# Layer 2 of one expert by seven block products in the first tile, with a new order of the first tile's steps

## The chip, the cores and the metric

The kernel runs on one core of a Trainium2 chip. A core has TensorE (PE, matmuls; its weight loads are listed as PEld), VectorE (DVE), ScalarE (ACT), GpSimd (POOL) and SyncE (SP, which here only starts DMA transfers). The engines run their own instruction streams in order and meet through semaphores; 16 DMA engines move data between HBM and the on-chip memory SBUF. PE writes its results to PSUM, in banks, from which DVE or ACT must take them ("evict") before the bank is used again.

The metric is the device time of one execution in microseconds (us). Before the change it is 486.61 us, the median of three runs (486.33 to 486.74).

## The reference

Linear attention is followed by a mixture of four expert networks, weighted by probabilities:

```python
def _attn_ref(q, k, v):                       # q, k, v: (8, 8, 576, 64)
    q_p, k_p = (phi(q), phi(k))               # phi(x) = elu(x) + 1
    kv = np.einsum('bhsd,bhse->bhde', k_p, v)
    z = np.sum(k_p, axis=2)
    num = np.einsum('bhsd,bhde->bhse', q_p, kv)
    den = np.einsum('bhsd,bhd->bhs', q_p, z)[..., None] + 1e-06
    return (num / den).astype(np.float32)
...
def _moe_ref(x, domain_probs, w1, w2):        # x: (4608, 512), w1: (4, 512, 1024), w2: (4, 1024, 512)
    p = domain_probs / (domain_probs.sum(-1, keepdims=True) + 1e-09)
    for e in range(E):
        h = np.maximum(x @ w1[e], 0.0)
        out += p[:, e:e + 1] * (h @ w2[e])
    return out.astype(np.float32)
```

The attention's output, with the heads side by side, is x: 8 batches of 576 tokens, 512 numbers each.

## The kernel before

**Tiles.** Of each batch 512 tokens form one tile; the 64 tokens left of each of the eight batches ("left") form a ninth. Tile 0 is batch 0. For each tile and each expert e, layer 1 (512 to 1024 numbers, then relu) and layer 2 (1024 to 512, scaled by the probability and summed over the experts in `acc`) are computed. While a tile is in the experts, the attention of the next batch is prepared.

**Block products.** From tile 1 on both layers are done by seven products of half-size blocks in place of the eight that a plain product of 2 by 2 blocks needs, at the price of sums of blocks. Layer 1: class `Block`, steps p1 to p7 with c22, for each half d of the hidden numbers; token sums `token_sum` (ts), weight sums `weight_sums` (s, on DVE). Layer 2: `layer2_product` (steps m, L786 on: seven products for each half of 256 tokens, 14 in all, four 128x256 matmuls each), with sums of the hidden numbers `hidden_sum` (hs, eight for a tile and expert, on POOL) and of the weights `weight_sums2` (t, four for an expert, on DVE). t.3 and s.3 change a block of the weights in place, and hs.2 a block of h.

**Tile 0** is different. Layer 1 of expert 0 is plain (`layer1_half`, steps L), layer 1 of experts 1 to 3 is by block products. Layer 2 is plain for all four experts: `layer2_part`, steps `y{e}.{ns}{part}`, four token groups ns of four parts each; a part is two matmuls of 128x512, and each group ends with one eviction into `acc`.

**Names of steps.** `p6.031` is step p6 of tile 0, expert 3, half 1; `y3.20` is expert 3, group 2, part 0; `m10.21` is tile 1, expert 0, product 2, token half 1; `hs10.03` is tile 1, expert 0, half 0, sum 3. `b1.` and `b2.` mark the attention of batches 1 and 2: k, q, v (ACT), km, qm (DVE), lk, lq, lv (the left rows), kv, qT, nd, xT, nl, xl (PE and an eviction).

**Loads.** q, k and v of batch 0 come by SP and ACT (lq0 to lq3, lk0 to lk3, lv0 to lv3), the probabilities by SP (lpr0 for tile 0, lpr for the rest; `emit_probs`, pr0 and pr1, norms them on DVE). POOL starts the transfers of the weights, which also cast them from fp32 to fp16: w1er is part r of w1 of expert e (four of 256 KB for expert 0, else two of 512 KB), w2er the same of w2; and those of batch 1 (k0 to k3, q0 to q3, v0 to v3, rk and rv for the left rows). Batch 2 comes by SP: `b1.load{i}` are its first six parts (load0 k0, load1 k1, load2 v0, load3 k2, load4 v1, load5 k3), `b2.load{i}` those after (load0 v2, load1 v3, load2 q0). `b1.loadlq` is the left q of batch 1, `b1.next` the left rows of batch 2. The raw parts share a pool of six buffers (`NRAW = 6`, tag "raw").

**The order** of all steps is written out by hand up to tile 1 in `CFG["EARLY"]`; after that steps go by a position (`put_at`). A step with several stages (a PE stage, then its eviction) stands in the list once for each: `advance` runs the step's generator on by one stage. The order of the list is the order in each engine's stream and in each engine's DMA queue.

Of the kernel before, what the change touches and what calls it, by code (L numbers as in the profile page):

```python
# [80 lines left out]
    "KC": ('AA', 'AV', 'VA', 'AA'),  # L81
    "XT": ('AA', 'AA', 'AV', 'AV'),
    "CUT": (((0, 2, 4),) * 4, ((0, 2, 4),) * 4),
    "MOVE": {"m83.10": 512.0, "m83.11": 512.0, "m83.20": 512.0, "m83.21": 512.0, "m82.41": 528.0},
    "WARM": (14, 3, 2, 1, 5),
    "BANK": {'qT0': 'py', 'qT1': 'b', 'nd00': 'py', 'nd00+': 'b', 'kv2': 'py', 'xT00': 'b', 'kv3': 'b', 'nd10+': 'b', 'L00': 'b', 'L10': 'py', 'nd01': 'b', 'xT01': 'py', 'nd11+': 'b', 'L20': 'e', 'L30': 'e', 'L01': 'e', 'L11': 'py', 'L21': 'py', 'L31': 'b', 'b1.qT3': 'py', 'b1.nd30': 'py', 'b1.nd21': 'b', 'b1.q1': 'b', 'b1.qT1': 'py', 'b1.nd01': 'py', 'b1.xT2': 'b', 'b1.nd11': 'py', 'b1.xT0': 'b'},
    "EARLY": (
        "lq2 lq3 lq0 lk0 qe0 ql0 ql3 qm0 kl0 lk1 lpr0 ke0 km0 qe2 ql2 qm2 lv0 ke1 kl1 km1 warm0 qT0 lv1 lk2 qe3 qm3 warm1 qT2 qT0 vc0 w100 warm2 kv0 vc1 qT2",
        "warm3 kv1 lk3 kv0 kv0 kl2 kv1 kl3 w102 kv1 nd01 lv3 nd01 warm4 xT11 xT01 ke2 km2 qT3 w103 vc3 lv2 ke3 vc2 nd00 w101 km3 xT01 w110 xT11 w111 kv3 k3 kv2",
        "qT3 lq1 nd00 qe1 xT00 w200 kv3 rk1 ql1 kv3 kv2 w201 qm1 L01 kv2 nd11 xT10 L31 qT1 v0 nd11 rv0 xT00 xT10 L10 xT21 rk0 xT21 v1 xT31 L11 qT1 xT31 nd10",  # L90
        "L01 L01 rv1 L31 w120 nd10 ts0.2 L00 ts0.0 xT30 ts0.1 xT20 L31 s0.0 L20 xT20 L30 xT30 L10 L10 L00 L00 L30 ts0.3 L30 p1.011 s1.0 p1.010 L11 L20 p1.010",
        "p2.010 s1.1 L20 w121 p2.010 p1.011 L21 L21 L21 s1.2 p6.010 p5.010 w210 L11 s1.3 p6.011 y0.30 p2.011 p6.010 p7.010 w211 p7.010 s0.1 p6.011 c22.010 v2",
        "y0.31 y0.00 p4.010 p2.011 y0.32 y0.33 p5.011 b1.k3 k0 pr0 y0.33 t0.0 t0.1 b1.km3 p7.011 p7.011 c22.011 y0.01 y0.02 y0.03 p4.010 b1.lk y0.20 y0.03 k2",
        "p4.011 s0.2 p3.010 p4.011 p3.011 y0.21 y0.10 y0.22 p3.010 y0.11 b1.v0 q1 k1 p1.021 y0.23 p1.021 p3.011 p1.020 s2.0 y0.12 v3 p2.021 b1.lv p1.020 t0.3",
        "s2.1 p2.020 s2.3 s2.2 y0.23 b1.v1 q0 t0.2 p6.020 p6.020 y0.13 p6.021 y0.13 y1.20 p7.020 y1.21 p2.020 p5.020 p7.020 w130 p2.021 y1.22 y1.23 t1.0 y1.10",
        "w131 p5.021 b1.v2 q3 b1.lkm y1.11 p6.021 b1.k0 b1.k2 b1.k1 w220 t1.1 t1.2 p7.021 y1.12 p7.021 c22.020 p3.020 y1.23 b1.v3 b1.km0 p4.020 p4.020 y1.00",
        "y1.01 q2 w221 y1.13 p4.021 b1.km2 b1.km1 b1.kv c22.021 p3.021 y1.02 y1.03 p1.030 p4.021 b1.q1 y1.30 y1.13 b1.load1 p1.031 b1.q0 p3.020 y1.31 p3.021",
        "p1.030 b1.qm1 b1.qT1 y1.32 y1.03 b1.qm0 s3.0 p1.031 w231 b1.qT0 s3.1 p2.030 y1.33 p6.030 b1.kv b1.qT0 p6.031 p2.031 b1.nd00 b1.nd01 b1.q3 p6.030 s3.3",
        "y1.33 p7.030 b1.loadlq p2.030 p5.030 b1.qm3 b1.qT3 p6.031 p7.030 w230 b1.qT1 b1.nd01 p7.031 p4.030 b1.qT3 s3.2 c22.030 b1.nd10 b1.nd11 b1.nd00 p2.031",
        "p3.030 b1.nd11 b1.nd10 p7.031 y2.00 y2.01 b1.nd30 p5.031 p4.031 p4.030 b1.next b1.nd31 b1.nd30 y2.20 b1.load0 b1.xT0 b1.lq b1.lqm b1.nd31 b1.q2 b1.qm2",  # L100
        "y2.21 b1.xT3 y2.02 c22.031 p4.031 b2.load2 y2.03 s0.3 b1.xT3 b1.qT2 y2.22 y2.23 b2.load1 b1.xT1 b1.load4 b1.load3 b1.load2 b1.qT2 b1.nd20 p3.031",
        "b1.xT1 p3.030 b1.nd21 y2.03 b1.xT0 b1.nd20 b1.nd21 y2.23 y2.10 y2.11 ts1.0 p1.101 p1.101 b1.load5 t1.3 b2.load0 t2.0 b1.xT2 y2.12 y2.13 b1.xT2 b2.k1",
        "ts1.1 lpr y2.30 y2.31 p1.100 p1.100 y2.32 y2.33 p3.031 p2.101 y3.20 y2.13 b2.km1 p6.100 b2.lk p2.100 t3.0 b2.load4 p2.101 p6.101 p6.100 p2.100 b2.lv",
        "ts1.2 p7.100 ts1.3 p7.100 b2.k0 y3.21 p5.100 y2.33 y3.22 t2.1 p4.100 y3.23 p6.101 p5.101 p4.100 p7.101 y3.30 c22.100 p3.100 b2.ones b1.qTl b2.v3 y3.00",
        "y3.01 p7.101 p4.101 b2.k2 b2.lkm y3.23 b2.km0 b2.load3 c22.101 b2.v1 y3.31 p3.100 t2.3 y3.32 p4.101 hs10.00 p3.101 b2.load5 y3.02 p1.110 b2.km2 y3.33",
        "p3.101 y3.03 b2.k3 b2.v0 b2.km3 b2.v2 b2.kv p1.110 y3.33 b2.load10 m10.21 b2.load7 p1.111 y3.03 y3.10 hs10.01 b1.qTl b2.q0 y3.11 p6.110 hs10.10",
        "hs10.02 y3.33 pr1 y3.12 y3.03 p1.111 m10.21 b2.q3 b2.load11 b2.qm0 y3.13 m10.51 hs10.11 p2.110 p6.111 p6.110 b2.q2 p2.111 m10.51 b2.qm3 y3.13 p2.110",
        "p6.111 t2.2 p7.110 m10.11 p5.110 m10.20 p7.110 b2.qm2 m10.11 b2.q1 c22.110 hs10.03 hs10.12 p7.111 m10.61 b2.qm1 t3.1 m10.20 p4.110 p4.110 p3.110",
        "p3.110 m10.50 p1.120 t3.2 b1.nl p2.111 p5.111 b3.load1 hs10.13 m10.61 m10.31 m10.31 m10.50 m10.10 p7.111 p4.111 b2.kv hs11.00 m10.10 m10.71 p1.120",
        "c22.111 t3.3 p6.120 m10.71 b2.lq b2.lqm p4.111 m10.60 b1.nl hs11.01 p3.111 p1.121 p6.120 y3.13 b2.load6 b2.qT m10.41 b2.qTl m10.60 m10.30 p2.120",  # L110
        "b2.nd1 p3.111 m10.41 m10.30 p7.120 b2.nd1 b2.nd0 hs11.10 y3.23 m10.70 m10.70 m11.21 hs11.11 p2.120 p5.120 m11.21 m10.40 p7.120 p4.120 hs11.03 p1.121",
        "p6.121 m11.20 m11.51 c22.120 p3.120 m10.40 b2.nd0 m11.20 p4.120 b3.k1 m11.50 m11.51 b3.km1 m11.11 p6.121 p2.121 m11.50 b2.nd1 b2.nd2 p3.120 p7.121",
        "m11.11 b2.nd3 b2.nd2 p1.130 hs11.02 p7.121 hs12.00 p2.121 b3.load0 b2.nd3 hs11.13 m11.10 m11.10 b2.next m11.61 m11.61 p5.121 p1.130 c22.121 p2.130",
        "m11.60 m11.31 p3.121 p6.130 m11.31 p4.121 b2.nd3 p6.130 hs11.12 m11.71 p4.121 p3.121 hs12.01 hs12.02 p2.130 m11.60 b2.nd4 hs12.10 p7.130 m11.71",
        "hs12.12 b2.nd5 p7.130 b2.nd2 b2.load8 m11.30 p5.130 p1.131 p1.131 m11.41 ts2.0 b2.nd4 b2.nd5 b2.nd5 m11.30 m11.41 m11.70 hs12.03 p6.131 p6.131 m12.20",
        "m11.70 m11.40 hs12.11 b3.ones c22.130 p4.130 p3.130 b1.xl p7.131 m12.21 p4.130 p7.131 m12.20 m11.40 b2.nl p2.131 b3.v0 p1.200 m12.21 b2.nl m12.50",
        "p2.131 m12.50 m12.51 p4.131 hs12.13 m12.51 ts2.1 p3.130 m12.10 m12.10 m12.11 m12.11 p5.131 p1.200 ts2.3 m12.60 m12.61 ts2.2 m12.60 b3.k0 m12.61",
        "c22.131 hs13.00 b2.load9 p4.131 p6.200",
    ),
}  # L120

# [2 lines left out]
def kernel(  # L124
# [642 lines left out]
        else:  # L767
            nc.vector.tensor_tensor(out=b12, in0=b22, in1=b12, op=AO.subtract)

    def hidden_sum(h, hs, i):  # L770

        a11, a21 = h[:, :, 0, 0:NH], h[:, :, 0, NH:NT]
        a12, a22 = h[:, :, 1, 0:NH], h[:, :, 1, NH:NT]
        if i != 2:
            hs[i] = pm.tile([P, 2, NH], FP16, tag=f"hs{i}", bufs=2, name=f"hs{i}")
        if i == 0:
            nc.gpsimd.tensor_tensor(out=hs[0], in0=a21, in1=a22, op=AO.add)  # L777
        elif i == 1:
            nc.gpsimd.tensor_tensor(out=hs[1], in0=hs[0], in1=a11, op=AO.subtract)  # L779
        elif i == 2:  # L780
            nc.gpsimd.tensor_tensor(out=a21, in0=a11, in1=a21, op=AO.subtract)  # L781
        else:
            nc.gpsimd.tensor_tensor(out=hs[3], in0=a12, in1=hs[1], op=AO.subtract)  # L783
# [220 lines left out]
    with tc.manual_schedule(  # L1004
# [46 lines left out]
        for e in range(E):  # L1051
            h0 = hT if e == 0 else [None, None]
            for d in range(2) if e else ():
                put_block(CFG["BLK"][2 * e - 2 + d], 0, e, d, h0)
            for i, pos in enumerate(CFG["L2P"][e]):
                put_at(pos, f"y{e}.{i // 4}{i % 4}", layer2_part, 0, e, i // 4, h0, i % 4, 4)
            for i in range(4):
                put_at(CFG["WS1"][e][i], f"s{e}.{i}", weight_sums, e, i)
                put_at(CFG["WS2"][e][i], f"t{e}.{i}", weight_sums2, e, i)
        base = CFG["BLK"][6]  # L1060
        units = [(j, e) for j in range(1, NTILES) for e in range(E)]
        for n, (j, e) in enumerate(units):
            h, hss = [None, None], [[None] * 4, [None] * 4]
            at = base + 2 * NSLOT * n
            for d in range(2):
                put_block(at + d * NSLOT, j, e, d, h)
            at += 2 * NSLOT + LAG

            def hsum(d, i, hT=h, hss=hss):
                hidden_sum(hT[d], hss[d], i)  # L1070

            for d in range(2):
                for i in range(4):
                    put_at(at + HSUM[d][i], f"hs{j}{e}.{d}{i}", hsum, d, i)
            order = L2ORD
            if n == len(units) - 1:
                order, at = (1, 2, 5, 6, 7, 3, 4), at + NSLOT
            for m in range(14):
                put_at(at + L2AT[m], f"m{j}{e}.{order[m // 2]}{m % 2}", layer2_product, j, e, h, hss, order[m // 2], m % 2)
# [71 lines left out]
```

## Time and profile before

| what | value |
|---|---|
| median of 3 runs | 486.61 us |
| span of the profiled execution, first to last instruction | 484.6 us |
| mean granted TensorE clock | 0.998 |
| PE, PEld busy | 474.4 us, 407.2 us |
| DVE, ACT, POOL busy | 377.3, 332.2, 358.3 us |
| bytes moved by DMA | 53.67 MB, of these 11.47 MB by POOL's queue (q0) |
| last landing of a weight part | 64.9 us |

The page gives the busy time of each engine, as a sum and in 40 slices, the DMA queues, the chain of work that ended last, and groups of instructions with their mean time and the idle time before them. The trace behind it can be asked for stages ("windows": busy time of each engine in a stretch), for the timeline of one engine (start, duration, engine, line, operation, out<-in; in brackets the idle time before and what ended it), and for waits. Line numbers are those of the kernel. A busy PE is not PE at its peak, as matmuls overlap; the distance from one start to the next is 0.109 us for a 128x256 matmul and 0.215 us for a 128x512 one.

### The profile page before, as it was taken

The page shows a single profiled execution, that of the slowest core. Times are in us where ns is not written, and L with a number is a line of the kernel's source. Part 1 is how long each engine was busy: PE and PEld are TensorE (multiplying, and loading weights), DVE is VectorE, ACT ScalarE, POOL GpSimd, SP SyncE. Part 2 cuts the span into 40 slices and gives each one's busy share as a digit, 9 for nine tenths or more (in the row PEclk, how much of TensorE's full clock was granted, in tenths as well). Part 3 has the DMA queues.
Part 4 walks back from the last instruction along what each step waited for, and adds up shares of the span by engine and source line. Part 5 has one row for each costly group of instructions (what it writes and reads, how often), then busy time and mean ns, then how long its engine had stood idle before and what let it go on. Part 6 is the DMA issues. An engine that isn't in the chain of part 4 may idle for free.

```text
span 484.6 us, 12013 instructions
## 1 busy us (share of the span) xinstructions
PE 474.4 (98%) x4565; PEld 407.2 (84%) x4565; DVE 377.3 (78%) x794; ACT 332.2 (69%) x662; POOL 358.3 (74%) x343
## 2 busy tenths in 40 slices
PE   6999999999999999999999999999999999999996
PEld 2766766898889888998889888988898888888885
DVE  5768987987868895888679886988687756775676
ACT  5689989956895599649884888478944565446530
POOL 5566044689966986789777977697769877987775
PEclk9999999999999999999999999999999999999999
DMA  8999987543445154523552446323221020002003
GB/s 293 216 217 254 233 204 201 134 109 88 123 144 111 42 156 150 120 53 115 172 135 56 114 133 157 77 77 106 69 59 28 7 93 2 1 0 89 2 1 87
DMA packets 79945, 53.67 MB, mean 111 GB/s; under 512 B 45152, under 2 KB 72608, under 8 KB 79888
## 3 DMA queue, kind: packets, MB, share of 16 engines
q1 hardware_dynamic: 69760, 40.43, 30.4%
q0 software_dynamic: 8896, 11.47, 12.3%
q10 hardware_dynamic: 1232, 1.02, 0.6%
q8 instruction: 35, 0.57, 0.5%
q14 instruction: 22, 0.18, 0.1%
HBM read 45.16 MB, written 9.44 MB: 113 GB/s over the span
## 4 chain that ended last, share of the span: by engine, by line
PE 90%; DMA 5%; DVE 2%; ACT 2%; issue 0%; POOL 0%; SPq 0%; ACTq 0%; DVEq 0%
PE py L810 38%; PE pb L868 24%; PE pe L868 18%; PE py L715 4%; DMA w<-in_moe_w_dram 2%; PE ph L655 1%; PE psum_nd L472 1%; DMA rawq<-in_q_dram 1%; DMA rawb<-in_q_dram 1%; DMA out_dram<-acc 1%; PE psum_kv L444 1%; PE pb L810 1%; PE pe L810 1%; DVE acc L706 0%; PE psum_nl L490 0%
## 5 line engine op out<-in xcount | busy, mean ns | idle before, releaser
L706 DVE SCALAR_TENSOR_TENSOR acc<-py,p_sb,acc 128x256 f32<-128x256 f32 (+1 forms) x382 | 182.2, 488 | 42.7 <-PE py L810 39.1
L852 DVE CUSTOM_DVE_ANT_0 h<-pe,u 128x512 f16<-128x512 f32 x140 | 96.1, 688 | 45.3 <-PE pe L868 28.0
L868 PEld LDWEIGHTS <-w 128*128 128x128 f16 x1120 | 108.9, 98 | 16.2
L777 POOL TENSOR_TENSOR hs<-h 128x512 f16<-128x512 f16 x64 | 74.7, 1167 | 56.9 <-DVE h L852 51.0
L810 PEld LDWEIGHTS <-h 128*128 128x128 f16 x1024 | 99.6, 98 | 12.2 <-issue 0.9
L810 PE MATMUL py<-w,h 128*128 128x256 f16 x744 | 106.4, 273 | 0.5 <-ACT acc L704 0.5
L879 ACT COPY u<-pb 128x512 f32<-128x512 f32 x140 | 82.4, 591 | 29.7 <-PE pb L868 27.8
L779 POOL TENSOR_TENSOR hs<-hs,h 128x512 f16<-128x512 f16 x64 | 74.1, 1157 | 26.8 <-PE py L810 24.3
L868 PEld LDWEIGHTS <-s 128*128 128x128 f16 x840 | 81.2, 98 | 12.6 <-DVE s L747 0.7
L868 PE MATMUL pb<-tt,w 128*128 128x256 f16 x560 | 83.8, 273 | 0.0
L810 PEld LDWEIGHTS <-hs 128*128 128x128 f16 x768 | 74.4, 98 | 8.8 <-issue 0.2
L783 POOL TENSOR_TENSOR hs<-h,hs 128x512 f16<-128x512 f16 x64 | 74.2, 1159 | 0.8 <-POOL h L781 0.5
L781 POOL TENSOR_TENSOR h<-h 128x512 f16<-128x512 f16 x64 | 74.6, 1165 | 0.1
L810 PE MATMUL py<-t,hs 128*128 128x256 f16 x496 | 74.1, 273 | 0.0
L901 ACT ACTIVATE h<-pe 128x512 f16<-128x512 f32 x70 | 41.9, 599 | 41.1 <-PE pe L868 40.5
L894 ACT COPY pe<-pb 128x512 f32<-128x512 f32 x70 | 40.0, 571 | 41.3 <-PE pb L868 15.8
L922 ACT ACTIVATE h<-pb 128x512 f16<-128x512 f32 x70 | 41.8, 599 | 6.3 <-PE pb L868 6.2
L868 PE MATMUL pb<-tt,s 128*128 128x256 f16 x280 | 41.9, 273 | 0.2 <-DVE s L747 0.2
L868 PE MATMUL pe<-tt,s 128*128 128x256 f16 x280 | 42.0, 273 | 0.0
L868 PE MATMUL pe<-xT,s 128*128 128x256 f16 x248 | 37.1, 273 | 0.0
L868 PE MATMUL pb<-xT,w 128*128 128x256 f16 x248 | 37.1, 273 | 0.0
L868 PE MATMUL pe<-xT,w 128*128 128x256 f16 x248 | 37.0, 273 | 0.0
(133 smaller groups left out, 594.6 us busy)
## 6 DMA issues: line engine op xcount, KB each, us to landing
out_dram<-acc SPq DMA_DIRECT2D x32, 256.0 KB, 2.5
w<-in_moe_w_dram POOLq DMA_DIRECT2D x14, 512.0 KB, 10.6
rawb<-in_k_dram SPq DMA_DIRECT2D x24, 256.0 KB, 3.1
rawb<-in_q_dram SPq DMA_DIRECT2D x24, 256.0 KB, 2.7
rawb<-in_v_dram SPq DMA_DIRECT2D x24, 256.0 KB, 2.8
w<-in_moe_w_dram POOLq DMA_DIRECT2D x4, 256.0 KB, 5.8
rawb<-in_k_dram POOLq DMA_DIRECT2D x4, 256.0 KB, 10.5
rl<-in_q_dram SPq DMA_DIRECT2D x16, 64.0 KB, 3.1
```

The source lines that it names most:

```text
L706: nc.vector.scalar_tensor_tensor(out=acc, in0=ps, scalar=pscal, in1=acc, op0=AO.mult, op1=AO.add)
L777: nc.gpsimd.tensor_tensor(out=hs[0], in0=a21, in1=a22, op=AO.add)
L779: nc.gpsimd.tensor_tensor(out=hs[1], in0=hs[0], in1=a11, op=AO.subtract)
L781: nc.gpsimd.tensor_tensor(out=a21, in0=a11, in1=a21, op=AO.subtract)
L783: nc.gpsimd.tensor_tensor(out=hs[3], in0=a12, in1=hs[1], op=AO.subtract)
L810: nc.tensor.matmul(out=ps, lhsT=lhsT(k), rhs=rhs[:, k], start=first and k == 0, stop=k == FH - 1, skip_group_check=True,)
L852: nc.vector._custom_dve(TENSOR_ADD_SAT, out=out, in0=ps, in1=u, s0=BIG, s1=0.0)
L868: nc.tensor.matmul(out=ps[:, kk], lhsT=lk(kc), rhs=rhs[:, kc], start=first and kk == 0 and kc == 0, stop=kc == 1, skip_group_check=True,)
L879: nc.scalar.copy(u, self.b)
L894: nc.scalar.copy(self.e5, self.b)
L901: nc.scalar.activation(self.h[:, :, 0, 0:NH], self.e5, AF.Relu)
L922: nc.scalar.activation(self.h[:, :, 1, 0:NH], self.b, AF.Relu)
```

## The change

Layer 2 of expert 3 in tile 0 is done by the 14 block products m03.* with eight sums hs03.* on POOL in place of the sixteen plain steps y3.*. `hidden_sum` takes the pair of halves and d, so that it can be called for both. `EARLY` is replaced as a whole, and reaches some 50 entries further; in it the loads have another order, and `lpr` and `pr1` stand early in tile 0.

```diff
+    "SEVEN": (3,),
...
     "EARLY": (
-        "lq2 lq3 lq0 lk0 qe0 ql0 ql3 qm0 kl0 lk1 lpr0 ke0 km0 qe2 ql2 qm2 lv0 ke1 kl1 km1 warm0 qT0 lv1 lk2 qe3 qm3 warm1 qT2 qT0 vc0 w100 warm2 kv0 vc1 qT2",
-        "warm3 kv1 lk3 kv0 kv0 kl2 kv1 kl3 w102 kv1 nd01 lv3 nd01 warm4 xT11 xT01 ke2 km2 qT3 w103 vc3 lv2 ke3 vc2 nd00 w101 km3 xT01 w110 xT11 w111 kv3 k3 kv2",
...
+        "lq2 lk1 lk2 lv1 lv0 lq0 lk0 lq3 lk3 lv2 ke0 lpr0 lv3 lq1 qe2 k3 kl0 km0 kl1 ke1 warm0 warm2 warm4 rk0 rk1 ql2 rv0 w100 qm2 km1 vc1 w102 vc0 ke2 kl2",
+        "qT2 kv1 km2 vc3 w101 w103 warm1 kv0 qe0 qe3 kv1 ke3 qT2 kv0 ql3 kv0 vc2 ql0 kv1 qm0 qm3 kl3 qT3 nd01 qT0 qT0 km3 nd01 qT3 kv2 warm3 kv3 nd00 ql1 kv2",
+        "w110 kv2 qe1 nd00 qm1 kv3 kv3 xT01 xT11 nd11 nd11 xT01 xT11 xT10 L11 xT00 L01 qT1 xT31 xT21 L21 xT10 qT1 xT00 xT21 xT31 nd10 L31 L01 w111 nd10 ts0.0",
+        "L30 ts0.1 ts0.2 pr0 s0.0 L21 xT20 xT30 w200 w201 b1.load1 b1.loadlq b2.load1 b1.load3 L01 xT30 xT20 L21 L00 L20 L31 L20 L31 L20 b1.lq L00 p1.010 L30",
+        "L10 L10 p1.011 w120 k1 w121 k0 lpr v0 ts0.3 b1.lqm s1.0 s1.1 s0.1 s1.3 w210 k2 v2 w211 v3 rv1 v1 q1 q0 w130 L00 L30 p1.010 p1.011 L11 p2.010 p2.011",
...
+        "p7.031 y2.00 y2.01 b1.nd30 b1.nd10 b1.qm2 b1.xT1 p3.030 b1.qT2 y2.20 y2.21 b1.nd31 y2.02 b1.nd00 y2.22 p4.031 b1.nd30 c22.031 p3.030 t3.0 y2.03 b1.qT2",
+        "b1.xT1 p4.031 p4.030 y2.23 p3.031 b1.nd00 b1.nd31 b1.xT0 b1.xT3 y2.03 y2.23 p3.031 t2.1 y2.30 b1.nd20 b2.lv b1.xT0 b1.xT3 hs03.00 y2.31 b1.nd21 y2.32",
+        "b1.nd21 b1.nd20 b2.k1 b2.k0 y2.33 y2.10 hs03.01 y2.11 y2.33 t3.3 b2.km1 b1.xT2 y2.12 y2.13 m03.20 p1.100 p1.101 y2.13 m03.20 m03.21 hs03.03 b1.xT2",
+        "hs03.10 ts1.0 ts1.1 b2.lk p1.100 p1.101 p6.100 m03.50 p2.101 p2.100 b2.lkm b2.km0 m03.21 t3.1 b2.ones ts1.3 b2.v0 b2.k2 hs03.12 hs03.11 hs03.13 ts1.2",
...
-    def hidden_sum(h, hs, i):
+    def hidden_sum(hT, d, hs, i):
+        h = hT[d]
...
-            for i, pos in enumerate(CFG["L2P"][e]):
-                put_at(pos, f"y{e}.{i // 4}{i % 4}", layer2_part, 0, e, i // 4, h0, i % 4, 4)
+            if e in CFG["SEVEN"]:
+                hss0 = [[None] * 4, [None] * 4]
+                for d in range(2):
+                    for i in range(4):
+                        put_at(90.0, f"hs0{e}.{d}{i}", hidden_sum, h0, d, hss0[d], i)
+                for m in range(14):
+                    put_at(91.0, f"m0{e}.{L2ORD[m // 2]}{m % 2}", layer2_product, 0, e, h0, hss0, L2ORD[m // 2], m % 2)
+            else:
+                for i, pos in enumerate(CFG["L2P"][e]):
+                    put_at(pos, f"y{e}.{i // 4}{i % 4}", layer2_part, 0, e, i // 4, h0, i % 4, 4)
```

In the new list, the SP queue's order is lq2 lk1 lk2 lv1 lv0 lq0 lk3 lv2 lpr0 lv3 lq1 b1.load1 b1.loadlq b2.load1 b1.load3 lpr b1.load0 b1.next b2.load2 b1.load4, the ACT queue's lk0 lq3, and POOL's k3 rk0 rk1 rv0 w100 w102 w101 w103 w110 w111 w200 w201 w120 k1 w121 k0 v0 w210 k2 v2 w211 v3 rv1 v1 q1 q0 w130 w131 q3 q2 w220 w221 w230 w231. Before, SP had lq2 lq0 lk1 lpr0 lv0 lv1 lk2 lk3 lv3 lv2 lq1 and then b1.load1, b1.loadlq and b1.next; ACT lq3 lk0; POOL w100 w102 w103 w101 w110 w111 k3 w200 rk1 w201 v0 rv0 rk0 v1 rv1 w120 w121 w210 w211 v2 k0 k2 q1 k1 v3 q0 w130 w131 q3 w220 q2 w221 w231 w230.

## What was predicted, blind

> **What bounds the kernel now.** I read the page's busy shares first, then the stages, then the chain of waits, last the rows of single lines. The page gives PE 474.4 us of a span of 484.6, at full granted clock in every slice, and the stages from 140 us on have PE busy without a break. So an edit counts in two ways only: by the PE work that it adds or removes, and by what it does to PE's idle time, and that lies in tile 0.
>
> ```profile
> PE 474.4 (98%) x4565; PEld 407.2 (84%) x4565; DVE 377.3 (78%) x794; ACT 332.2 (69%) x662; POOL 358.3 (74%) x343
> ```
> ```profile
> 3.00:12.20 9.20, 6.39 (x65) 2.85 (x64) 5.78 (x12) 5.10 (x12) 6.27 (x7) 1.00 1.09 372
> 12.20:23.60 11.40, 10.54 (x147) 8.74 (x147) 8.19 (x22) 7.77 (x20) 6.61 (x10) 1.00 1.17 216
> 23.60:52.30 28.70, 28.70 (x239) 19.71 (x237) 23.20 (x40) 25.78 (x51) 15.10 (x21) 1.00 1.18 238
> 52.30:65.00 12.70, 12.46 (x111) 8.93 (x110) 12.14 (x29) 11.06 (x23) 0.15 (x1) 1.00 1.17 212
> 65.00:76.00 11.00, 11.00 (x80) 7.38 (x79) 9.81 (x17) 10.00 (x21) 5.16 (x5) 1.00 0.56 172
> ```
>
> The columns are stage, length, busy time of PE, PEld, DVE, ACT, POOL, clock, DMA share and GB/s written. The DMA engines are full (share over 1) from 3 to 65 us. The weight loads read fp32 and write fp16, so 212 to 238 GB/s written is near twice that read, like the 372 of the plain loads. Tile 0 is thus a race between PE and one full set of DMA engines, and it is close:
>
> ```profile
> 23.68 0.69 DVE L745 TENSOR_TENSOR s<-w 128x1024 f16<-128x1024 f16 x1 [1.21 <-DMA w<-in_moe_w_dram]
> ```
> ```profile
> 42.60 9.66 DMA w<-in_moe_w_dram
> ...
> 52.36 0.70 DVE s L745
> ...
> 53.08 0.70 DVE s L747
> ...
> 53.83 1.05 PE pb L868 x8
> ```
>
> The first row is s1.0, which waited for w111 (landed 23.6). The second group is the chain: w131 lands at 52.26, s3.0 and s3.1 follow, then p6.030, and PE stood about 0.4 us. Expert 3's weights have no slack at all, expert 1's about 1 us.
>
> **The products.** A plain step is two 128x512 matmuls, a block product four 128x256:
>
> ```profile
> 64.32 0.86 PE py L715 x4
> ...
> 467.62 0.87 PE py L810 x8
> ```
>
> Expert 3 had 32 matmuls of 0.86/4 = 0.215 us, 6.9 us; it gets 14 products of 4 at 0.87/8 = 0.109 us, 6.1 us. **PE: -0.8 us.** Only this is certain, and it is less than what a measurement can tell from no change (0.2%, about 1 us).
>
> **What the products need.** DVE: 4 evictions of 742 ns become 14 of 480 ns, +3.8 us; pr1's four instructions (about 1.0 us) move from tile 1 into tile 0, and the wait of 2.69 us of POOL's hs10.00 for them goes; what ends last there next is c22/p3 as in every other unit. t3.0 to t3.3 are in both kernels, only earlier. Cover for the 3.8 us: DVE is busy 9.81 of 11 us in 65 to 76 and 12.4 of 15 in 75 to 90 (stages of five us), so some 3.8 us are idle there; without it PE would wait for a PSUM bank, up to 3.8 us. POOL: 8 sums of 1.16 us, 9.3 us, in a stretch where it sits idle 5.6 us before 76.64 and 0.15 us busy in 52 to 65. In the new order POOL runs hs03 and ts1 mixed: up to ts1.1 it has six operations, 7 us, from c22.030 on, and p6.100, which needs ts1.1, stands 7.4 us of PE work behind c22.030. Bounds 0 to 1 us of PE idle, I take **+0.2**, as the sum fits just in time.
> [...]
>
> **The order: loads.** Here is the loss. Before, SP issues its eleven first loads by 7.1 us and then stands at b1.load1 for a raw buffer:
>
> ```profile
> SPq L319 <- DMA rawb<-in_k_dram: 35.2, 1, 35.2
> ```
>
> It goes out at 44.6. In the new order q0 to q3 and k3 take five of the six raw buffers of the pool and b1.load1 the sixth, so nothing holds it: b1.load1, b1.loadlq, b2.load1, b1.load3 and lpr stand right behind lq1 on SP and go as SP's earlier loads land, between 8 and 14 us. None of it is wanted before tile 0's second half. On POOL's queue k3, rk0, rk1 and rv0 are moved past w100. All this is in line before w110 (issued about 14 us, as vc3 on POOL now waits for lv3, SP's tenth load).
> The price, by 256 KB at 372 GB/s = 0.7 us: k3 0.7, three left loads of 64 KB 0.8 (by bytes at 238), three raw loads 2.1, the two left q 0.5: 4.1 us. lpr has small packets; before, its three DMAs landed over 1.2 us: 0 or 1 us, depending on whether it gets in line in time; I take 1. In the old trace w102 and w110 landed 0.6 us each later than back to back, and a longer line uses that up: 4.1 + 1.0 - 1.2 = 3.9, w111 at 27.5 in place of 23.6. Bounds: 25.1 if SP's loads stand behind the weights (POOL's own 1.5 us alone), 28.7 with lpr and no slack.
> [...] The trace's 372 GB/s is used.
>
> What it does to PE: I count PE work along each order (block products and layer-1 steps 0.436 us, plain steps 0.432, transposes 0.22, kv 0.73, nd 0.11 a pair, warm-up 0.216 a matmul). Before, p6.010 has 17.9 us ahead of it and starts at 26.25; p6.030 has 45.1 and starts at 53.83: 27.6 us for 27.2, the stall of 0.4 being the rest. So the count holds. In the new order p6.010 has 18.35 ahead. It needs s1.1, which before ended 1.5 us after w111's landing: 27.5 + 1.5 = 29.0. Without a stall it would come at 26.25 + 0.45 = 26.7. L01's second half (w101) and L21's (w103) wait first, for the same lateness. **+2.3 us** (bounds 0 and 3.5).
>
> Later: p6.030 comes at 29.0 + 45.13 - 18.35 = 55.8. Ahead of w131 are only b2.load1, b1.load3 and lpr more than before (b1.load1 and loadlq were there already): 52.3 + 1.4 to 2.4, so p6.030 could run at 55.3 to 56.3. No new stall, the old one is absorbed: **-0.4**.
> t2.0 and t3.0 are moved up on DVE, to PE counts 49.2 and 53.4 from 56.7 and 61.7, so about 59.5 and 64.2 us. They need w220 and w230. After w131 (about 54.2) come q3 and q2 (1.4), w220 (2.55): 58.1, w230 63.2, and up to 3.7 us later if b1.load0, the six left loads and two raw loads of SP get between. While DVE stands at t3.0, y2.03, y2.23 and p3.031 wait for their evictions and xT0 for nd00; PE has about 1.5 us of work before it needs one of them. Bounds 0 to 2.5 us, I take **+0.6**.
>
> Sum: -0.8 + 0.2 + 2.3 - 0.4 + 0.6 = +1.9. The profiled execution has 484.6 us of span, 2.0 below the median of 486.6 of the runs; the difference is added to the latter: **488.5 us**.
>
> **Rivals.**
> 1. The loads are not in the weights' way: 485.4. If POOL's transfers come first wherever both queues have work, w111 lands at 25.1, p6.010 runs at 26.7 by PE's own count, and -0.8 - 0.4 remain. Against it: SP's load issued at 44.61 landed at 52.45, between w131 and q3 of POOL, not behind the four weight parts that POOL had in line. It decides as soon as w111 lands before 25.2. The start can help it: k1, v1 and v0 are loaded ahead of q0 and q3, so kv1 (11.03 before, behind vc1) can come a us or two earlier, but that counts only if the weights are there. Chance 0.2.
> 2. The second half bites too: 491.5. SP's loads released by 50 to 57 us push w220 and w230 back by the full 3.7 us; DVE stands at t2.0 and t3.0, PE idles 2.5 us, and POOL's chain is late by 1 us. For it: DMA share 1.17 up to 65 us. Chance 0.2.
> 3. Half of the line is hidden: 486.6. w111 at about 26.3, a lag of 1.2 us, against -0.8 and -0.4. Chance 0.15.
> That the products do not replace the plain ones can't be: the steps y3 are gone from the order and m03 take their places.
>
> **Numbers.** Forecast (487.6 to 490.2) 0.45, rivals 0.2, 0.2, 0.15. Faster by over 0.2% needs under 485.6: rival 1, 0.2. Within 0.2% (485.6 to 487.6): rival 3, 0.15. Slower 0.65. The range goes from 485.2, rival 1's place, to 492.0, just over rival 2.
>
> **What would show it.** Right: SP issues three raw loads and the left q before 15 us; w111 lands after 26.5 us; PE is idle two us or more between 18 and 30 us, with DMA w named before s1.0 or ph; p6.010 near 29. Wrong: PE without gaps from 18 us on, or w111 before 25. The step at t3.0 shows as DVE idle at L762, ended by DMA w, near 64 us. If the time falls under 486, the loads step failed.

## The result, and the profile after

The changed kernel takes 497.79 us (median of 4 runs, 497.73 to 499.23) against 486.65 us of the kernel before on the same chip (486.33 to 486.74): ratio 1.0234, 95% interval 1.0219 to 1.025. That is 11.1 us slower, where 1.9 us were forecast.

The profiled execution has a span of 495.9 us, mean granted clock 0.988. Three lines of its page (busy time; the granted clock and the DMA share in 40 slices of 12.4 us):

```profile
PE 479.7 (97%) x4589; PEld 413.0 (83%) x4589; DVE 380.6 (77%) x804; ACT 332.3 (67%) x662; POOL 367.3 (74%) x351
...
PEclk9599999999999999999999999999999999999999
DMA  9999973525347233732453244523231020002003
```

VectorE has 3.3 us more to do and GpSimd 9.0 us more, near the 3.8 and 9.3 us counted in the forecast for the evictions and sums. The clock was 9 in every slice before; now the second slice shows 5.

The same five stages as in the table of before (columns as there):

```profile
3.00:12.20 9.20, 6.80 (x43) 2.82 (x41) 5.12 (x10) 3.81 (x8) 5.76 (x7) 1.00 1.08 349
12.20:23.60 11.40, 9.51 (x118) 7.77 (x119) 5.97 (x16) 6.32 (x17) 7.42 (x11) 0.55 1.20 256
23.60:52.30 28.70, 28.46 (x253) 20.59 (x250) 22.96 (x46) 25.18 (x51) 12.98 (x19) 1.00 1.19 232
52.30:65.00 12.70, 12.70 (x121) 9.57 (x114) 12.48 (x26) 11.06 (x22) 0.31 (x1) 1.00 1.20 229
65.00:76.00 11.00, 10.77 (x82) 6.91 (x80) 10.71 (x23) 8.97 (x19) 9.44 (x9) 1.00 0.54 136
```

PE did 118 matmuls from 12.2 to 23.6 us where it did 147, at a clock of 0.55. From 52 to 76 us VectorE is busy 23.2 of 23.7 us, GpSimd in 65 to 76 us 9.4 of 11 where it was 5.2.

To see where time went I took *PE's lost time* at a step: the start of its first matmul in the trace, less the PE work issued before it (each matmul at its steady distance, 0.109 us for 256 columns, 0.216 for 512). It compares two orders at the same place:

| at the step | before, us | after, us | added since the row above |
|---|---|---|---|
| p6.010 | 8.1 | 13.0 | 4.9 |
| y2.10 | 8.8 | 13.9 | 0.2 |
| p1.120 | 9.8 | 15.7 | 0.9 |
| after tile 1's last gap in the new order, 130 us | 9.9 | 20.2 | 4.4 |
| last matmul | 11.8 | 23.7 | 1.6 |
| PE work in all | 468.0 | 467.2 | -0.8 |

The column sums to 12.0 - 0.8 = 11.2, against 11.1 measured. So this table says where time went; it does not say why, and the experiments show that a loss undone at one place can come back at another.

**The start.** SP's queue in the changed kernel, as forecast, issues three raw loads before 15 us:

```profile
10.33 0.38 SPq L322 DMA_DIRECT2D rawb<-in_k_dram  x1
...
12.54 0.64 SPq L322 DMA_DIRECT2D rawb<-in_v_dram  x1
13.29 0.40 SPq L322 DMA_DIRECT2D rawb<-in_k_dram  x1
```

w111 landed at 27.58 us (forecast 27.5), but PE came to it later still, so it was not what PE waited for. The timelines of PE and of GpSimd (start, duration, line, operation, in brackets the idle time and what ended it):

```profile
10.26 0.48 PE L609 MATMUL psum_kv<-vpos,kpos 64*64 64x65 f16 x18 [1.69 <-DVE vpos L576]
...
12.58 0.47 PE L609 MATMUL psum_kv<-vpos,kpos 64*64 64x65 f16 x18 [1.09 <-DVE kvz L620]
```
```profile
15.39 0.67 POOL L576 CAST vpos<-vrawt 128x576 f16<-128x576 f32 x1 [4.31 <-DMA vrawt<-in_v_dram]
```

The first inputs are late: v3 landed at 15.34 us (11.55 before), q1 at 17.14 (12.20). GpSimd stands 4.3 us at v3's copy, and the weights behind it on its queue with it. And the granted clock falls; stretches of 2 us, with PE's busy time first and the clock in the last column but two:

```profile
12.00:14.00 2.00, 1.10 (x25) 1.00 (x26) 1.64 (x6) 1.96 (x7) 0.00 (x0) 0.75 1.16 270
14.00:16.00 2.00, 2.00 (x31) 1.34 (x29) 1.15 (x3) 1.37 (x3) 0.61 (x1) 0.50 1.15 283
...
20.00:22.00 2.00, 2.00 (x13) 1.47 (x12) 0.58 (x1) 0.37 (x1) 2.00 (x4) 0.50 1.25 200
22.00:24.00 2.00, 2.00 (x23) 1.83 (x22) 0.49 (x2) 0.86 (x2) 1.12 (x2) 0.69 1.25 210
```

From 20 to 22 us PE is busy throughout and gets 13 matmuls done.

**Tile 1.** A part of the chain of waits (start, duration, what), and PE's waits from 95 to 135 us (sum, times, longest):

```profile
116.45 0.45 PE py L814 x4
116.90 0.03 issue
116.92 0.89 DVE acc L709 x2
117.81 0.04 issue
117.85 0.60 PE py L814 x4
```
```profile
PE py L814 <- DVE acc L709: 1.9, 3, 1.0
PE py L814 <- ACT acc L707: 1.1, 2, 0.8
```

A product (m11.30) waits for the eviction of the one before it in its half of the bank, because that one's PE part stands too close ahead in the new order. Seven such gaps, 0.30 to 1.13 us, make 4.4 us. Before, this stretch had none over 0.15 us.

### The profile page after: what moved, and what is told of

Read it like the earlier page. It is cut to its first block, busy times and chain, and to the rows that moved or that the text cites. A ratio compares the mean times of both kernels' runs of the same rounds, so it can differ in the third digit from the quotient of the medians.

```text
span 495.9 us, 12080 instructions
## 1 busy us (share of the span) xinstructions
PE 479.7 (97%) x4589; PEld 413.0 (83%) x4589; DVE 380.6 (77%) x804; ACT 332.3 (67%) x662; POOL 367.3 (74%) x351
## 3 DMA queue, kind: packets, MB, share of 16 engines
q0 software_dynamic: 8896, 11.47, 11.9%
## 4 chain that ended last, share of the span: by engine, by line
PE 87%; DMA 7%; DVE 4%; ACT 1%; issue 0%; SPq 0%; ACTq 0%; DVEq 0%
PE py L814 37%; PE pb L872 23%; PE pe L872 17%; DMA qT<-qp 4%; PE py L718 3%; DVE acc L709 2%; PE ph L658 2%; DMA rawq<-in_q_dram 2%; DMA vraws<-in_v_dram 1%; PE psum_nd L475 1%; PE psum_kv L447 1%; PE pb L814 1%; PE pe L814 1%; DVE h L856 0%; DVE kp L355 0%
## 5 line engine op out<-in xcount | busy, mean ns | idle before, releaser
L709 DVE SCALAR_TENSOR_TENSOR acc<-py,p_sb,acc 128x256 f32<-128x256 f32 (+1 forms) x392 | 185.4, 485 | 46.8 <-PE py L814 42.9
L781 POOL TENSOR_TENSOR hs<-h 128x512 f16<-128x512 f16 x66 | 77.1, 1168 | 74.0 <-DVE h L856 61.5
L856 DVE CUSTOM_DVE_ANT_0 h<-pe,u 128x512 f16<-128x512 f32 x140 | 96.0, 688 | 46.1 <-PE pe L872 29.5
L814 PEld LDWEIGHTS <-h 128*128 128x128 f16 x1056 | 102.8, 98 | 14.0 <-issue 2.0
L814 PE MATMUL py<-w,h 128*128 128x256 f16 x768 | 110.1, 273 | 1.2 <-ACT acc L707 0.8
L783 POOL TENSOR_TENSOR hs<-hs,h 128x512 f16<-128x512 f16 x66 | 76.7, 1164 | 24.4 <-PE py L814 22.1
L814 PEld LDWEIGHTS <-hs 128*128 128x128 f16 x792 | 76.7, 98 | 12.7 <-issue 4.1
L814 PE MATMUL py<-t,hs 128*128 128x256 f16 x512 | 76.8, 273 | 1.0 <-DVE acc L709 1.0
L787 POOL TENSOR_TENSOR hs<-h,hs 128x512 f16<-128x512 f16 x66 | 76.7, 1164 | 1.1 <-POOL h L785 0.5
L785 POOL TENSOR_TENSOR h<-h 128x512 f16<-128x512 f16 x66 | 76.8, 1163 | 0.0
L898 ACT COPY pe<-pb 128x512 f32<-128x512 f32 x70 | 40.2, 576 | 39.5 <-PE pb L872 14.7
L926 ACT ACTIVATE h<-pb 128x512 f16<-128x512 f32 x70 | 41.7, 597 | 9.5 <-PE pb L872 9.5
L872 PE MATMUL pe<-tt,s 128*128 128x256 f16 x280 | 41.7, 273 | 0.0
L814 PE MATMUL py<-w,hs 128*128 128x256 f16 x256 | 38.4, 272 | 2.2 <-DVE acc L709 1.7
```

The costliest lines, as they stand in the source:

```text
L709: nc.vector.scalar_tensor_tensor(out=acc, in0=ps, scalar=pscal, in1=acc, op0=AO.mult, op1=AO.add)
L814: nc.tensor.matmul(out=ps, lhsT=lhsT(k), rhs=rhs[:, k], start=first and k == 0, stop=k == FH - 1, skip_group_check=True,)
L856: nc.vector._custom_dve(TENSOR_ADD_SAT, out=out, in0=ps, in1=u, s0=BIG, s1=0.0)
L872: nc.tensor.matmul(out=ps[:, kk], lhsT=lk(kc), rhs=rhs[:, kc], start=first and kk == 0 and kc == 0, stop=kc == 1, skip_group_check=True,)
L898: nc.scalar.copy(self.e5, self.b)
L926: nc.scalar.activation(self.h[:, :, 1, 0:NH], self.b, AF.Relu)
```

## The experiments

Times are medians beside runs of the kernel before on the same chip; "+x" is the difference of the two. Orders are given as moves in `EARLY`.

### The start

**Filler matmuls** (warm), to hold the clock:

```diff
-    "WARM": (14, 3, 2, 1, 5),
+    "WARM": (14, 12, 2, 5, 8),
```

> The changed kernel with more filler matmuls in the start (14, 12, 2, 5, 8 of them in the five places in place of 14, 3, 2, 1, 5), nothing else. Theory clock (most of the start's loss is the granted clock of 0.50 from 13 to 23 us, which follows PE's idle time): the clock stays above 0.9 up to 24 us and PE's lost time at p6.010 falls from 13.0 to 9.5 to 11 us, the filler counted as lost. Theory loads (PE waits there for inputs that land late in any case): the clock rises, the lost time stays within 0.5 us of 13.0. The time falls with it to 495 us in the first, stays at 497 to 498 us in the second.

496.25 us, +9.5, ratio 1.0184 (1.0162 to 1.0205). The clock shows 9 in every slice, p6.010 starts at 29.5 us in place of 31.4. By the work of the changed kernel that is a lost time of 11.1 us, just above the 11 of theory clock: a full clock gives back 1.9 of the 4.9 us, with the filler counted as lost.

**SP's and GpSimd's early loads put back** (loads_late):

```diff
-... lv3 lq1 qe2 k3 kl0 ... warm4 rk0 rk1 ql2 rv0 w100 ...
+... lv3 lq1 qe2 kl0 ... warm4 ql2 w100 ...
-... L01 w111 nd10 ... w200 w201 b1.load1 b1.loadlq b2.load1 b1.load3 L01 ...
+... L01 w111 k3 nd10 ... w200 w201 rk0 rk1 rv0 L01 ...
-... b1.nd10 b1.nd11 b1.load0 b1.next ...
+... b1.nd10 b1.nd11 b1.load1 b1.loadlq b1.load0 b1.load3 lpr b1.next ...
```

The steps b1.lq, b1.lqm and pr1, which use what is loaded, move back with the loads, and b2.load1 to just before b2.load0.

> The changed kernel with its early loads put back behind the first ones: on SP b1.load1, b1.loadlq, b2.load1, b1.load3 and the probabilities stand just before b1.load0 and b2.load0, on POOL k3 after w111 and rk0, rk1, rv0 after w201; the rest of the order is as changed. Theory loads (the extra transfers share the DMA engines with the first inputs): v3 and q1 land by 12.5 us, PE's idle time before 13 us is gone and with it the low clock, lost time at p6.010 8.1 to 9.5 us; 493 to 494 us if the later stalls stay as they are. Rival (the changed order of the evictions in the start holds PE, not the loads): lost time at p6.010 stays over 12 us. The forecast's step for these loads (2.3 us, by the weights): 10.7 us.

498.73 us, +11.9, ratio 1.0242 (1.0211 to 1.0273). Lost time at p6.010 is 11.8 us: near the rival's bound, but v3 and q1 still land at 13.3 and 15.5 us, now behind w100 and w102. The time is not shorter at all: at p1.100 of the profiled execution, the longest of the four with 500.64 us, 16.0 us are lost, 2.2 more than in the changed kernel.

**w100 and w102 put back too** (start_loads):

```diff
-... ql2 w100 qm2 km1 vc1 w102 vc0 ke2 ...
+... ql2 qm2 km1 vc1 vc0 w100 w102 ke2 ...
```

> The run with the early loads put back (loads_late: lost time at p6.010 11.8 us, v3 and q1 still landing at 13.3 and 15.5 us behind w100 and w102, and w103 to w111 issued 2 us later than before because GpSimd's queue stands at vc3 for v3), with w100 and w102 moved on GpSimd's queue behind vc0, as they stand in the kernel before. Theory loads (the start is late by the order of the first transfers, the low clock follows from it): v3 and q1 land by 12.5 us, w110 by 23 us, the clock stays full and lost time at p6.010 is 8.1 to 9.5 us. Rival (the changed order of the steps on ScalarE and VectorE in the start keeps PE late by itself): 10.5 us or more.

Lost time at p6.010 is 8.45 us, the clock is full: all but some 0.4 us of the start's loss comes from the order of its first transfers. Yet the time is 498.39 us, +12.2, ratio 1.0248 (1.0231 to 1.0266). The 4.6 us are lost again by 74 us.

**GpSimd's first transfers alone put back, SP's left early** (start_pool; b1.load1 to lpr stay early):

```diff
-... lv3 lq1 qe2 k3 kl0 ... rk0 rk1 ql2 rv0 w100 qm2 km1 vc1 w102 vc0 ...
+... lv3 lq1 qe2 kl0 ... ql2 qm2 km1 vc1 vc0 w100 w102 ...
-... L01 w111 nd10 ... w200 w201 b1.load1 ...
+... L01 w111 k3 nd10 ... w200 w201 rk0 rk1 rv0 b1.load1 ...
```

> The changed kernel with only GpSimd's first transfers put back: w100 and w102 behind vc0, k3 behind w111, rk0, rk1 and rv0 behind w201; SP's early loads and the probabilities stay where the change has them, so nothing is wanted later that lands later. Theory carried (a start that is early by itself brings the end forward): lost time at p6.010 8.5 to 9.5 us and 4 us of it still there at y2.10: 493.5 to 494.5 us. Theory VectorE (from 40 us on VectorE is busy without a break in the changed order and sets when y2.10 comes, 70 to 72 us in every run with it): p6.010 is early, y2.10 comes within 1.5 us of 71.0, 496 to 498 us.

Lost time at p6.010 is 9.0 us, y2.10 comes at 69.8 us where it came at 71.0: of 4.1 us regained, 1.2 are left. 496.38 us, +9.9, ratio 1.0204 (1.0168 to 1.0241). VectorE's timeline of this run and of the changed kernel at t3.0 shows why:

```profile
64.84 1.18 DVE L765 TENSOR_TENSOR t<-w 128x1024 f16<-128x1024 f16 x1 [1.84 <-DMA w<-in_moe_w_dram]
```
```profile
65.92 0.68 DVE L765 TENSOR_TENSOR t<-w 128x1024 f16<-128x1024 f16 x1
```

w230 lands at 64.8 us here and at 64.4 in the changed kernel: the DMA engines are full until then in both runs (share 1.20 to 1.23 from 55 to 65 us), though PE starts earlier here. VectorE stands 1.8 us at t3.0 for it, and the evictions behind. With the late start it comes there without a wait. PE in start_pool waits for what stands behind t3.0 on VectorE (from 26 to 85 us, besides other waits):

```profile
PE psum_xT L515 <- DVE x_sb L463: 0.9, 1, 0.9
PE py L718 <- DVE acc L709: 0.4, 1, 0.4
```

So of the gain of 4.1 us some 1.6 go at t3.0, and the rest of what is lost in smaller waits before it. Time and y2.10 are those of theory VectorE, but VectorE is not busy without a break: it stands for w230.

**The start alone** (start_only: 167 entries of the changed order, then those of before):

```diff
-... p2.010 s1.1 L20 w121 p2.010 p1.011 L21 L21 L21 s1.2 p6.010 ...
+... p2.010 p2.011 p2.010 L10 p6.010 p6.011 p6.010 s1.2 p5.010 ...
```

> The kernel before with the start of the changed one alone: the changed order up to the second stage of p6.010 (167 entries, with the early loads and the load of the probabilities), then what is left in the order of before, with plain layer 2 in tile 0. Theory carried (PE's lost time is carried to the end where PE bounds): lost time at p6.010 near 13, 4.9 us slower than before, 491.5 us. Theory slack (the loads that went early let the later ones land earlier, and VectorE, not PE, sets the pace of tile 0's second half): less than half of it stays, 487 to 489 us.

500.67 us, +14.7, ratio 1.0306 (1.0288 to 1.0325): neither. GpSimd's queue stands 13.7 us at a raw load (L320, from 42.4 us on), w130 and w131 behind it land at 63.6 and 66.1 us, PE stands 4.8 us at p2.020 and 2.5 us at p1.030. The start's loads and the order of the next 60 us are one thing; half of it is worse than all.

**The old start under the new rest** (cut144: entries up to p6.010 as before, then the rest of the changed order):

```diff
-... L11 p2.010 p2.011 p2.010 L10 p6.010 p6.011 ...
+... L21 L21 L21 s1.2 pr0 b1.load1 ... w130 p2.011 p6.010 p6.011 ...
```

> The changed kernel with the start undone: the first 144 steps stand as in the kernel before (up to p6.010), then come the steps of the changed order that are left, in its order; probabilities are still loaded in tile 0 and the seven products are kept. Theory 1 (the start's delay is carried to the end): PE's lost time at p6.010 falls from 13.0 back to about 8.1 us and the end comes 4.9 us earlier, 492.9 us. Theory 2 (work after the start is bound by VectorE, the start's delay is only absorbed there): p6.010 comes 4.9 us earlier, but the stalls after 70 us grow by as much, 496 to 498 us. My forecast's own step for the start was 2.3 us: 495.5 us.

498.67 us, +12.2, ratio 1.0251 (1.0235 to 1.0266). Lost time at p6.010 is 10.9 us, so it comes only 2.2 us earlier where both theories took 4.9, and at y2.10 14.7. The outcome is nearer to theory 2, though a new stall of PE of 2.5 us before 41.7 us (a raw load of k lands at 40 us) has a part in it.

### Tile 1's order

**Tile 1 as before, the rest changed** (tile1_old):

```diff
-... p3.101 b2.q2 hs10.00 p6.110 p1.111 p2.110 m10.20 p6.110 p2.110 hs10.10 ...
+... p3.101 b2.q2 m03.30 t1.3 t2.3 m03.40 hs10.00 b2.load10 m03.30 m10.21 b2.load7 ...
```

> The changed kernel up to the first hidden sum of tile 1 (hs10.00, about 85 us); from there on tile 1's steps stand in the order of the kernel before, with the last evictions of the seven products in between. Theory order (the stalls between 95 and 131 us, 4.4 us in sum, belong to the new order of tile 1, in which a product follows too closely on the eviction that it waits for): they are gone, PE's lost time grows by less than 0.8 us from p1.120 to the end of the stretch, 493.0 to 494 us. Theory work (tile 0's products leave VectorE behind, and any order of tile 1 stalls): 2 to 4 us of stalls stay between 85 and 131 us, 496 to 498 us.

494.22 us, +7.4, ratio 1.0145 (1.0125 to 1.0165). From p1.120 to 131 us 0.1 us are lost, as theory order has it. So 3.7 of the 11.1 us are this order. The gain is less than the 4.4 us of gaps, since 1.9 us of stalls come at m10.21 and m10.51, ahead of p1.120, which the changed kernel does not have there.

**Tile 1 as changed, the rest as before** (tile1_new; the last plain parts y3 read a block of w2 that t3.3 has already changed, so its output is another):

```diff
-... hs10.00 p3.101 b2.load5 y3.02 p1.110 b2.km2 y3.33 ...
+... p1.110 p3.101 b2.q2 hs10.00 p6.110 p1.111 p2.110 m10.20 ...
```

> The kernel before up to its first hidden sum of tile 1 (plain layer 2 in tile 0, its start, its loads), from there on tile 1 in the changed order, with the last y3 parts in between. Theory order (the stalls of 4.4 us between 95 and 131 us belong to the new order of tile 1): they appear here too, 490.5 to 491.5 us. Theory work (they come from what tile 0 leaves behind): at most 1 us of them, 486.5 to 488 us.

496.94 us, +10.9. More than either theory: where the two orders are joined, three stalls of 2.3, 1.1 and 2.2 us come between 80 and 88 us, and they are mine. But the seven gaps are there in the same places and sizes, 4.5 us, with plain layer 2 in tile 0 (PE's waits from 95 to 135 us of this run):

```profile
PE py L813 <- DVE acc L708: 1.9, 3, 1.0
PE py L813 <- ACT acc L706: 1.2, 2, 0.8
```

They are in all runs with this order and in none without it: order, not work.

### The seven products

**Plain layer 2 in the changed order** (plain_new):

```diff
-    "SEVEN": (3,),
+    "SEVEN": (),
```

> The changed order with plain layer 2 parts y3 in the places of the product steps, hidden sums of that expert left out, t3.0 to t3.3 after the last y3. Theory P (the products' vector work makes the stalls after 78 us): PE's lost time from p1.100 to m10.20 falls by 1.7, up to m12.20 by 3 to 4, and PE has 0.8 more to do: 494 to 496 us. Theory O (the order alone makes them): stalls stay, PE has 0.8 more to do: 498.6 us.

498.84 us, +12.4, ratio 1.0259 (1.0238 to 1.028): theory O by its number. The 1.1 us at the products are gone, but t3.0 to t3.3, which I had put in a row behind the last y3, make one of 2.6 us at m10.50. The run does not separate the two. But it shows that the changed order is slow without the products as well: even with those 2.6 us taken off, an estimate, it stays 9.8 us behind the kernel before.

**The old order up to p1.100** (cut393) and **the products in the old order** (seven_old; in it m03.60, m03.40, m03.71 and m03.41 are added into the bank before the product ahead of each is taken from it, so its output is another):

```diff
-... b1.next b1.nd31 b1.nd30 y2.20 b1.load0 b1.xT0 ... y3.20 y2.13 ...
+... b1.next b1.nd31 b1.nd30 y2.20 b1.load0 lpr b1.xT0 ... m03.20 y2.13 ...
```

> The order of the kernel before up to tile 1's first p1.100 (the load of the probabilities right after b1.load0, as the buffers need it), then what is left in the changed order, with the seven products. Theory A (the start and the second half after p1.100 are separate prices): start and tile 0's middle gone, -4.9 - 0.2; the stalls from 80 us on (1.7 in the m03 stretch, 3.0 at m10 to m12, 5 later) stay: 492.5 us. Theory B (the later stalls come from VectorE work that the changed order of tile 0's middle leaves behind): they go too, 486 to 488 us.

> The kernel before with the seven products alone: its order, m03 in the places of the y3 parts, hidden sums where the token sums end, t3 and the probabilities earlier as the buffers need it. Theory P (the products' vector work makes new stalls): -0.8 for PE, +1.7 to +4 for stalls from the m03 stretch on: 487.5 to 490 us. Theory O (the stalls of the changed kernel come from its order): -0.8 and no stall over 0.5 us that the kernel before lacks: 485.8 us.

499.55 us (+13.1) and 495.94 us (+9.5). Both have a mistake of mine: the load of the probabilities stands behind b1.load0 on SP and lands at about 69 us. From cut393's chain:

```profile
66.38 2.38 DMA praw<-in_moe_domain_probs_dram
...
69.16 0.99 DVE p_sum L267
```

VectorE stands there for pr1, and PE 5.3 and 3.7 us. The runs only show that the probabilities must be loaded early.

**The products alone, probabilities early** (seven_only):

```diff
-... b1.k3 k0 pr0 ... p4.011 s0.2 p3.010 p4.011 ... y3.20 ... y3.13
+... b1.k3 k0 lpr pr0 ... p4.011 s0.2 p3.010 pr1 p4.011 ... t3.0 p3.031 t2.1 b2.lv hs03.00 ... m03.20 p1.100 ... m03.41
```

> The kernel before with the seven products alone: its order up to p1.100, the probabilities loaded after k0 and spread after p3.010, then the changed order of the steps of that stretch up to hs10.00, then the order of the kernel before for tile 1. Theory order: the products cost what they cost in the changed kernel's stretch (1.4 us of stalls) and save 0.8 us: 486.6 to 487.5 us. Theory products (VectorE's added work holds PE back whatever the order): 489 us or more.

495.33 us, +8.5, ratio 1.0165 (1.0123 to 1.0207). Theory products. Lost time is 8.9 us at y2.10 as before, and 17.9 at p1.120 where it was 9.8. PE's longest waits from 65 to 95 us are those of products for evictions:

```profile
PE py L812 <- DVE acc L707: 4.7, 3, 2.6
```

**The same with weight sums moved out** (seven_tuned) and **in an order of its own** (seven_late):

```diff
-... t3.0 p3.031 t2.1 b2.lv hs03.00 y2.32 b2.k0 y2.33 hs03.01 y2.33 t3.3 b2.km1 m03.20 p1.100 y2.13 m03.20 ...
+... p3.031 t3.0 b2.lv hs03.00 y2.32 b2.k0 y2.33 hs03.01 y2.33 b2.km1 m03.20 p1.100 y2.13 t3.3 m03.20 ...
...
+... p1.100 p1.100 y2.32 y2.33 p3.031 y2.33 hs03.00 hs03.10 t3.0 p2.101 m03.20 y2.13 t3.3 b2.km1 p6.100 m03.21 ...
```

> The kernel with the seven products alone, as run before (495.3 us), with five weight sums that tile 1 wants only at m11 and m12 (t1.3, t2.0 to t2.3, 0.7 to 1.4 us each on VectorE) moved out of the stretch, behind hs10.01, c22.110, p3.110, c22.111 and p3.111, and t3.0 and t3.3 put behind the evictions p3.031 and y2.13. Theory VectorE (VectorE's work in the stretch sets its pace): the stalls of 4.0 us at m03.20 and m03.21 shrink by 3 us or more, 491 to 492.5 us. Theory chain (the hidden sums on GpSimd or the banks of the products hold PE): under 1 us is gained, 494.5 to 495.5 us.

> The kernel before with the seven products alone once more, in an order made by what the runs showed: tile 1's first block products go first and one m03 step stands behind each of them, GpSimd does hs03.00 and hs03.10, then ts1.2 and ts1.3, then the other sums, each product stands where its sums are ready by GpSimd's 1.15 us an operation, y2.33 and y2.13 are evicted ahead of the sums of weights, and t1.3 and t2.0 to t2.3 come in tile 1. Theory place (a product costs nothing where its sums and its eviction have time, the 8.5 us came from the bubble in which PE had nothing but them): 485.8 to 487.5 us. Theory load (VectorE and GpSimd have not the time for the products in tile 0 in any order): 490 us or more.

494.25 us, +8.2, ratio 1.0163 (1.0139 to 1.0187), and 494.36 us, +8.2, ratio 1.0166 (1.0151 to 1.0181). In seven_tuned the stalls at m03.20 and m03.21 shrink from 4.0 to 1.4 us, and 2.5 us come at m03.50 and m03.31, which now wait for hidden sums. seven_late has its eight stalls in other places, 7.5 us in sum. Three orders, one price. GpSimd's timeline and PE's waits in seven_late:

```profile
68.00 2.26 POOL L779 TENSOR_TENSOR hs<-h 128x512 f16<-128x512 f16 x2
70.21 1.61 POOL L851 TENSOR_TENSOR tt<-xT 128x512 f16<-128x512 f16 x1
71.78 1.60 POOL L851 TENSOR_TENSOR tt<-xT,tt 128x512 f16<-128x512 f16 x1
73.34 2.74 POOL L781 TENSOR_TENSOR hs<-hs,h 128x512 f16<-128x512 f16 x2
```
```profile
PE py L812 <- DVE acc L707: 2.2, 4, 0.8
PE py L812 <- ACT acc L705: 2.0, 1, 2.0
PE pe L870 <- DVE h L854: 1.0, 1, 1.0
PE py L812 <- POOL tt L851: 0.9, 1, 0.9
```

GpSimd runs without a break from 66.9 to 81 us, and VectorE from 80 to 86. PE waits for each of the three other engines in turn.

**Parts of it.** The early steps without products (t3_early: lpr, pr1 and t3.0 to t3.2 moved, y3 kept):

> The kernel before, plain layer 2 kept, with the probabilities loaded after k0 and spread after p3.010, and t3.0, t3.1, t3.2 moved up to where the seven products need them (after p3.031, p2.100 and c22.100). What remains of the seven products' price is then evictions, hidden sums and their order. Theory A (the sums that must be ready before the products hold VectorE): half or more of the 8.5 us of the run with the products alone, 490 to 492 us. Theory B (the 14 evictions and the sums on GpSimd beside VectorE make it): 486.5 to 488 us.

486.18 us, +0.2, ratio 1.0002 (0.9992 to 1.0012). The probabilities and the early sums of weights cost nothing. On top of this, GpSimd's part and VectorE's part each by itself:

```diff
+                if e == E - 1:
+                    hss0 = [[None] * 5, [None] * 5]
+                    for d in range(2):
+                        for i in range(4):
+                            put_at(90.0, f"hs0{e}.{d}{i}", hidden_sum, h0, d, hss0[d], i)
...
-            add_acc(j, e, ns, py, slice(0, Dm), e == 0)
+                add_acc(j, e, ns, py[:, 0:DH], slice(0, DH), False)
+                add_acc(j, e, ns, py[:, DH:Dm], slice(DH, Dm), False)
+                for _ in range(2 if ns > 1 else 1):
+                    nc.vector.scalar_tensor_tensor(out=accs[j, ns][:, 0:DH], in0=py[:, 0:DH], scalar=0.0, in1=accs[j, ns][:, 0:DH], op0=AO.mult, op1=AO.add)
```

> The run t3_early (plain layer 2, probabilities and t3.0 to t3.2 early, as fast as before) with the eight sums hs03 on GpSimd added, where seven_late has them; nothing reads them, and the third of each half writes beside the hidden numbers and not into them. Theory GpSimd (its eight operations of 1.15 us before tile 1's own sums make the price of the products in tile 0): PE's lost time at p1.120 grows from 9.8 to 13 us or more, 489.5 to 494 us. Theory evictions (the products wait for VectorE, the sums fit beside): under 12 us there, 486 to 488 us.

> The run t3_early with VectorE's part of the products alone: each of the four plain evictions of expert 3 in tile 0 is done in two halves of 128x256, and six more additions of that size that add nothing follow, so that there are the 14 operations of the seven products, 3.8 us more than in t3_early; no hidden sums. Theory evictions: PE's lost time at p1.120 grows by 3 us or more, 489 us or more. Theory GpSimd: VectorE has the room that the forecast saw (3.8 us idle between 65 and 90 us), under 1 us, 486 to 487 us. If both runs stay under 488, the price is in the products' own chain (sum, product, eviction, next product of the bank) and in no engine's load.

488.57 us, +2.3, ratio 1.0046 (1.0031 to 1.0061), and 488.01 us, +1.7, ratio 1.0032 (1.0019 to 1.0045). Lost time at p1.120 is 12.1 and 11.2 us. PE's longest waits, first in the run with GpSimd's sums, then in the one with VectorE's evictions:

```profile
PE pb L870 <- POOL tt L851: 1.1, 1, 1.1
```
```profile
PE py L715 <- DVE acc L728: 0.8, 1, 0.8
```

In the first PE waits for tile 1's token sums, which come later on GpSimd. Both results lie between their theories. Each of the two costs something, so the room that the forecast saw was not there; together they are 4.0 of the products' 8.2 + 0.8 = 9.0 us, if they add up, which no run shows. The rest, about 5 us, shows only when products hang on sums and evictions; that this chain makes it is argued from the waits, not shown by a run of its own.

**Start and tile 1 as before, tile 0's middle as changed** (start_tile1: start_pool's edit on tile1_old):

> The same with tile 1 in the order of the kernel before as well, so that of the change the middle of tile 0 with the seven products is left. Theory carried: the gains of both add, 497.8 - 4 - 3.5, 490 to 491 us. Theory VectorE: only tile 1's share is gained, 493.5 to 494.5 us.

494.63 us, +8.2, ratio 1.0158 (1.0128 to 1.0188). Theory VectorE was near: putting the start right adds nothing to tile 1's gain. What is left equals the price of the products alone, but it lies elsewhere. By the measure of the table PE has lost 4.2 us more than the kernel before at y2.10, ahead of every product, and 7.1 us more at p1.120; in seven_only it is 0.1 and 8.1 us. So the equal numbers do not show that the products make all of it.

## Why the prediction was wrong

Only the direction held. Two steps failed: what the products need, and the order of tile 1, which the sum puts at nothing without a reason. By its steps:

- **The products, PE -0.8 us.** Right: PE has 0.8 us less to do.
- **What the products need, +0.2 us.** This step failed. It saw 3.8 us of room on VectorE between 65 and 90 us and let GpSimd's sums fit "just in time". Put alone into the kernel before, the products cost 8.2 to 8.5 us in three orders. The extra work was counted rightly (3.8 us and 9.3 us); wrong was to set the idle sum of a 25 us stretch against it. GpSimd's sums alone cost 2.3 us, VectorE's evictions alone 1.7, and in the three orders PE waits in turn for a sum, an eviction and the product before. In the changed kernel itself PE comes to this stretch 5.9 us later than before (p1.100 at 73.4 us), and loses only 1.5 us at products (0.4 at m03.21, 1.1 at m03.61). GpSimd's sums are in time there: hs03.00 begins at 66.1 us, behind p3.030 and not c22.030, and p6.100 follows 9.0 us later without a wait. The 7.4 us of PE work that the forecast counts from c22.030 to p6.100 are about 11.6 by its own unit costs.
- **The order: loads, +2.3 us.** The loads went as forecast and w111 landed as forecast, but PE lost 4.9 us, not to the weights but to the first inputs, which the same early transfers and w100 and w102 put back, and a full clock gives back 1.9 of it. Undone beside the products this is worth 1.2 us (start_pool) or nothing (start_tile1 beside tile1_old), since PE loses it again before y2.10, in part at t3.0. What it is worth without the products no run shows.
- **Later, -0.4 us.** The old stall at p6.030 is indeed gone.
- **t2.0 and t3.0, +0.6 us.** The sign named for it, VectorE idle at that line until w near 64 us, is absent in the changed kernel and present with 1.8 us as soon as the start is in time: the step was real, and hidden by the start.
- **Not in the sum at all: tile 1's order.** 3.7 us by undoing it (tile1_old), 4.4 us of gaps by the trace, and the same gaps appear when it is put into the kernel before (tile1_new). The forecast read the new order as far as its loads and tile 0, and never put a product of tile 1 beside the eviction that it waits for.

So 3.7 of the 11.1 us are tile 1's order, shown both ways. The other 7.4 us are the rest of the change, the start and tile 0 with the products. There the prices of single changes are no shares: the products alone cost 8.2 to 8.5 us, the start undone alone gives 1.2, both the start and tile 1 undone leave 8.2 with half of it ahead of the products, and the products taken out of the changed order gain nothing (plain_new, +12.4, or 9.8 without the stall of 2.6 us there). A loss at one of these places covers a loss at another, and how the 7.4 us divide among them stays open. None of the versions made is faster than the kernel before. Left open are also three waits of PE for the transposes qT at 160, 211 and 263 us, 0.4 to 0.9 us each and 1.8 in sum, which come and go between the runs; no run was made for them.

## What to carry to other kernels

Here a saving of 0.8 us on the bounding engine was lost many times over, because its operands come from engines that are idle only in pieces: put the chain of each new operation (sum, operation, eviction, next operation) in order of time, and do not add up idle time. When the order of a hand-written schedule changes, look at every pair of operations that share a bank, also where nothing else has changed. A table of where time is lost names places; only undoing a place shows whether it is a price or cover for another one, and two undoings that give the same time need not have removed the same waits.

## What the hardware showed that I had not expected

The granted clock fell to 0.50 for about 10 us (0.75 in the mean from 12 to 14 us, 0.69 from 22 to 24) after two idle stretches of PE of 1.69 and 1.09 us, with 0.5 and 0.8 us of matmuls between them, and came back at about 23 us. With the filler matmuls of warm it stayed full (9 in every slice). In seven_only it was 0.87 in the mean from 70 to 75 us and 0.78 from 75 to 80, after stalls of 2.7 and 1.3 us (PE busy 3.56 us from 65 to 70 and 2.75 from 70 to 75). How much idle time it takes no run shows.

In seven_late GpSimd's sums of 1.15 us took up to 1.61 us beside VectorE's sums of weights, and these 1.0 to 1.3 us in place of 0.67 (four of five from 69 to 89 us; the one at 73.28 us took 0.67). That the one makes the other longer is read from their overlap in time alone. The kernel before has a sum of 1.61 us too (at 86.55 us, beside a sum of weights of 1.38 us at 85.77), and what part of the products' price this makes no run shows.
